# First norm's second step moved late, masks of v copied by ScalarE, and the raw loads of v put in order

## The chip, the cores and the metric

One core of a Trainium2 chip runs the whole program. The metric is the device time of one execution in microseconds (us). Engines are named as the profile names them: PE (matmuls) with PEld (its weight loads), DVE (VectorE), ACT (ScalarE), POOL (GpSimd), SP (SyncE, which here only issues transfers). PEclk is the clock granted to PE as a share of full speed.

## The reference

Four sequences of 576 tokens with 8 heads of 64 go through causal attention with a decay, then a normed MLP of 512 to 2048 to 512, then a gated spatial MLP. This case concerns the first two parts:

```
scores = scale * q @ k.T + (cum[:, None] - cum[None, :])      # cum: running sum of log f, causal mask
attn   = softmax(scores) @ v
xn     = (x - mean(x)) / sqrt(var(x) + 1e-06) * g_ln
x      = x + max(xn @ w_ch1, 0) @ w_ch2
```

The MLP's weights come as 64-bit numbers.

## The kernel before

Tokens are worked in blocks of 256 (`BLOCKS`), features on the partitions. Each block passes through an attention function (`attention32` for the first two blocks, `attention1` for the next two, `attention` later), a norm (`norm`) and the MLP (`mlp`); every block is an MLP group of its own here (group 0, group 1, ...). The MLP walks over `NF` = 16 weight blocks: a first product into `ph` (L840), a relu `hh` on ACT (L851), and a second product into the accumulators `acc` (L825), two weight blocks behind. There are 2 banks for `ph`, 2 for `acc`, 1 for `av`, and 3 buffers of `hh`.

Group 0 runs in f32 while its weights arrive: SP loads 64-bit words (`raw`, 3 buffers, L657 and L660), ACT and DVE narrow them (L641, L642 on ACT; L643, L644, L645 on DVE, the last into `wt`), PE adds up their squares (L692 into `gram`). From the squares `scales` derives scales (L710 to L716), and `make16` writes the weights as pairs of 16-bit parts (L723 on ACT, L726 on DVE). Groups from 1 on use these: their input is split into `xh` (L803, ACT) and `xl` (L804, DVE), and each product is made of three.

The norm of block 0 is cut in two. Its first step puts g and the mean into `xg0` (L755), from which group 0 can start. The second step (`self.rest`) finds the deviation: centring `xT` (L758), squares `sq` (L764 on ACT, summed by POOL in L768 and L769), a mean on PE (L736 into `av`), then `y` (L772, L773 on ACT and L774 to L776 on DVE). Group 0's products are multiplied by this `y` only at its end (L874), which also frees `acc` for group 1. `gscale` finds the scale `gs` of g that L803 and L804 use (L249 to L255).

A table of due positions (`REST`, `DEC`, `CONV`, ... in units of groups) sets in which order `run` writes the work. A scheduler in the framework then orders each engine's instructions; `self.after(later, earlier)` ties two of them in order, with `self.marks` for the named ones, and `high_priority` puts work first. In `attention32`, four steps `p` each make masks of scores (L440), an exponential (L442), a sum, a reciprocal and a diagonal matrix (L463 to L467), a transposing product (L473), and the product with `vm` (L485), which holds v twice under a mask. `attention1` runs eight units of scores (L518, L523, L525, L319, L534), a transfer that transposes (L535, `PT`<-`P`) and the product with v (L543 into `av`). `vnorm` loads v once more (`vraw`, L294 and L298) for its squares (L304).

Of the kernel before, what the change touches and what calls it, by code (L numbers as in the profile page):

```python
# [1 line left out]

# [4 lines left out]
F32 = mybir.dt.float32  # L7
# [6 lines left out]
AF = mybir.ActivationFunctionType  # L14
ALU = mybir.AluOpType
# [3 lines left out]
P = 128  # L19
# [6 lines left out]
TOK = 256  # L26
# [31 lines left out]
PACE = (1, "x3", "split", "split", "split")  # L58
LOWAT = (1, "x3", "split")
SUMS = 14  # L60
REST = 0.1
SQ = (1, 3, 4, 5, 6, 8, 9, 10, 12, 13, 14, 16)
SOON = 5
WSC, MAKE, VN = 0.76, 0.765, 0.82
# [24 lines left out]
class Kernel:  # L89
# [126 lines left out]
    def decays32(self, behind):  # L216


        nc, cum, lg, n = self.nc, self.cum, self.lg, B * H
        added = nc.vector.tensor_tensor(out=lg[:, P : P + 1], in0=lg[:, P : P + 1], in1=cum[:, P - 1 : P], op=ALU.add)  # L220
        self.after(added, behind)
        ones = self.ones[:n, :1].broadcast_to([n, S - P])
        return nc.vector.tensor_tensor_scan(out=cum[:, P:], data0=ones, data1=lg[:, P:], initial=0.0, op0=ALU.mult, op1=ALU.add)

    def decays16(self):

# [169 lines left out]
    def attention32(self, b, xT):  # L396
        nc, at, bufs = self.nc, self.at, BUFS0
        mm = nc.tensor.matmul

        def bank(tag):  # L400
            return self.bank(tag).rearrange("p (b u w) -> p b u w", b=2, u=2)

        def four(tag):
            return at.tile([P, 2, 2, P], F32, tag=tag, name=tag, bufs=bufs[tag])

        tags = ("s2", "s2", "av") if b else ("acc", "ph", "av")
        qka = self.qka0 if not b else at.tile([P, NP, 2, 2, 2 * P], F32, tag="qk", name="qk", bufs=bufs["qk"])
        vra = at.tile([P, 2, DM], F32, tag="vr", name="vr", bufs=bufs["vr"])
        vm = self.vm
        loads = []  # L410
        for p in range(NP):
            loads.append(nc.sync.dma_start(out=qka[:64, p], in_=self.qk0[b : b + 2, p].rearrange("n d u s -> d u n s")))
            if b and p == 1:
                for r in range(2):
                    row = qka[64 + r : 65 + r].rearrange("r p u n s -> r (p u n) s")
                    nc.sync.dma_start(out=row, in_=self.decay[b * H : (b + 2) * H, r])
        loads.append(nc.sync.dma_start(out=vra, in_=self.v[b : b + 2, :P].rearrange("b p d -> p b d")))
        for u in range(2):
            us = slice(64 * u, 64 * u + 64)
            v = vra.rearrange("p n (q w) -> p n q w", w=P)  # L420
            nc.gpsimd.tensor_copy(out=vm[:, :, :, u, us], in_=v[:, :, :, us])
        if b == 0:
            for x, y in zip(loads, loads[1:]):
                self.after(y, x)
            self.marks["loads"] = loads[-1]
        yield

        def scores(p):
            qk = qka[: 66 if b else P, p]
            ps, e = bank("s2" if p > 1 else tags[0]), four("e")  # L430
            st = at.tile([P, 2, 4], F32, tag="st", name="st", bufs=bufs["st"])
            for n, u, c in four_:
                ins = mm(ps[:, n, u], lhsT=qk[:, u, n, :P], rhs=qk[:, u, n, P:], start=True, stop=True, skip_group_check=True)
                if b and p == c == 0:
                    self.after(ins, self.first)
            if not b and p % 2:
                self.fill(FILLS[p // 2], ins)
            for n, u, c in four_:
                mn, sm = st[:, 0, c : c + 1], st[:, 1, c : c + 1]
                masked = nc.vector.tensor_tensor_reduce(  # L440
                    out=e[:, n, u], in0=ps[:, n, u], in1=self.mask[:, 512:], scale=-0.125, scalar=3e38, op0=ALU.add, op1=ALU.min, accum_out=mn)
                ex = nc.scalar.activation(e[:, n, u], e[:, n, u], AF.Exp, bias=mn, scale=-1.0, accum_out=sm)  # L442
                if b:
                    self.after(masked, self.marks["third" if p else "second"])
                    self.after(ex, self.marks["split"])
            if b:
                nc.scalar.activation(st[:, 1], st[:, 1], AF.Copy, bias=1e-9)
                nc.vector.reciprocal(st[:, 1], st[:, 1])
            else:
                self.masked = masked  # L450
            return e, st

        four_ = [(n, u, 2 * n + u) for n in range(2) for u in range(2)]
        ahead = []
        for p in range(NP):
            for i in range(len(ahead), min(p + 2, NP) if b else NP):
                ahead.append(scores(i))
                yield
            e, st = ahead[p]

            ps, pt, diag = bank(tags[1]), four("PT"), four("diag")
            if not b:
                total = nc.vector.tensor_scalar(out=st[:, 1], in0=st[:, 1], scalar1=1e-9, scalar2=None, op0=ALU.add)  # L463
                self.after(total, self.masked)
                self.masked = None
                nc.vector.reciprocal(st[:, 1], st[:, 1])
            drawn = nc.vector.tensor_tensor(  # L467
                out=diag.rearrange("p n u w -> p (n u) w"), in0=self.ident.unsqueeze(1).broadcast_to([P, 4, P]),
                in1=st[:, 1].unsqueeze(2).broadcast_to([P, 4, P]), op=ALU.mult)
            if not b:  # L470
                self.masked = drawn if p != 1 else self.decays32(drawn)
            for n, u, c in four_:
                ins = mm(ps[:, n, u], lhsT=e[:, n, u], rhs=diag[:, n, u], start=True, stop=True, skip_group_check=True)  # L473
            if not b and p < NP - 1:
                self.fill(FILLS[2], ins)
            if b or p % 2:
                copied = nc.scalar.activation(pt, ps, AF.Copy)
            else:
                copied = nc.vector.tensor_copy(out=pt, in_=ps)
            if not b:  # L480
                self.done.append(copied)
                self.marks[f"PT{p}"] = copied
            pav = bank(tags[2] if b else ("av", "s2", "acc", "s2")[p])
            for n, u, c in four_:
                ins = mm(pav[:, 0, n], lhsT=vm[:, n, p, u], rhs=pt[:, n, u], start=u == 0, stop=u == 1, skip_group_check=True)  # L485
            if not b and p == NP - 1:
                self.fill(FILLS[3], ins)
            copied = nc.scalar.activation(xT[:, p].rearrange("p (n w) -> p n w", n=2), pav[:, 0], AF.Copy)
            if not b:
                nc.scalar.activation(self.xg0[:, p].rearrange("p (n w) -> p n w", n=2), pav[:, 0], AF.Copy, scale=self.gT[:, p : p + 1])  # L490
            self.marks.setdefault(f"x{p}", copied)
            if p == 1:
                xs = self.mo_sum(xT)
            elif p == 2:
                nc.vector.tensor_tensor(out=xs, in0=xs, in1=xT[:, 2, :], op=ALU.add)
            yield
        return xs
# [166 lines left out]
    def load_w(self, j):  # L664

        nc = self.nc
        if j not in self.raw:
            self.load_raw(j)
        raw, w = self.raw.pop(j), self.wt[:, j + 2]
        low = self.st.tile([P, 2 * DM], U32, tag="low", name="low", bufs=2)  # L670
        joined = self.joined if 0 < j < 4 else None
        for hf in range(1 if j else 2):
            c = slice(0, 2 * DM) if j else slice(hf * DM, hf * DM + DM)
            first = self.narrow(raw[:, c], w[:, c], low[:, c], self.marks["split"] if hf else joined if j else self.marks["PT2"])
            for ins, pace in ((first, PACE), (self.low, LOWAT)):
                at = "x3" if hf else pace[j] if j < len(pace) else NP + j - len(pace) if ins is first else None
                if at is not None:
                    self.after(ins, self.marks[at] if isinstance(at, str) else self.done[at])
        if j == 1:
            self.marks["second"] = self.joined  # L680
        if j == 2:
            self.marks["third"] = self.joined

# [55 lines left out]
    def norm(self, x, s, y, whole, end, c):  # L739
# [11 lines left out]
        if c is not x:  # L751
            self.fill(FILLS[4], self.averaged)
            for t in range(NK):
                xg = self.xg0[:, t]
                self.marks["split"] = nc.vector.scalar_tensor_tensor(out=xg, in0=pm, scalar=self.gN[:, t : t + 1], in1=xg, op0=ALU.mult, op1=ALU.add)  # L755
            yield
        for t in range(NK):
            centred = nc.vector.tensor_tensor(out=c[:, t, :], in0=x[:, t, :], in1=pm, op=ALU.subtract)  # L758
# [667 lines left out]
```

## Time and profile before

| | us |
|---|---|
| median of 3 runs (lowest, highest) | 781.63 (781.2, 781.8) |
| the profiled execution | 784.81 |
| span of its trace | 782.8 |

| engine | busy us | share of the span |
|---|---|---|
| PE | 752.6 | 96% |
| DVE | 557.2 | 71% |
| ACT | 522.2 | 67% |
| POOL | 70.5 | 9% |

The span runs from the first to the last instruction; the execution took 2.0 us more. The profiled execution is 3.2 us above the median of the runs. A busy share is a mean over stages that differ much, so the stage that a change touches has to be read by itself. Times of records overlap by a little: an ACT record of 0.71 us, say, can be followed by the next one 0.61 us after its start.

### The profile page before, as it was taken

What the parts mean: (1) busy time and instruction counts of PE and PEld (TensorE: products, weight loads), DVE (VectorE), ACT (ScalarE), POOL (GpSimd) and SP (SyncE); (2) the same over time, 40 slices, a digit from 0 to 9 for tenths busy, and PEclk for the clock granted to TensorE, in tenths of its full rate; (3) what the DMA queues carried; (4) which work ended last, traced back from release to release, by engine and by line L of the source; (5) the groups of instructions that cost most, each with busy time, mean ns of one, the idle gap of its engine ahead of it and who ended that gap; (6) DMA issues with size and microseconds to landing.
All of it is one profiled execution on the core that took longest, in us unless ns stands there. A gap on an engine that the chain in (4) does not pass through costs nothing.

```text
span 782.8 us, 16313 instructions
## 1 busy us (share of the span) xinstructions
PE 752.6 (96%) x5966; PEld 578.3 (74%) x5966; DVE 557.2 (71%) x1508; ACT 522.2 (67%) x1317; POOL 70.5 (9%) x104
## 2 busy tenths in 40 slices
PE   7889998999999989999999999999999999999998
PEld 6778877877877867778888888544447678668676
DVE  7899698667599889979869946587525672654624
ACT  6888598667588888878759834485416743756543
POOL 5210101012101001110101100100021000000000
PEclk9999998999999999999999999999999999999999
DMA  9968994266679998987994955730034310100101
GB/s 256 279 239 284 296 182 77 55 189 102 186 154 202 183 207 152 211 198 153 178 204 108 132 80 196 192 118 29 1 80 75 102 63 1 39 23 17 47 1 61
DMA packets 164099, 104.69 MB, mean 134 GB/s; under 512 B 106146, under 2 KB 151298, under 8 KB 164020
## 3 DMA queue, kind: packets, MB, share of 16 engines
q1 hardware_dynamic: 157784, 96.60, 51.2%
q0 software_dynamic: 5376, 5.54, 5.0%
q10 hardware_dynamic: 860, 1.52, 0.6%
q8 instruction: 47, 0.77, 0.4%
q14 instruction: 32, 0.26, 0.1%
HBM read 64.37 MB, written 15.11 MB: 102 GB/s over the span
## 4 chain that ended last, share of the span: by engine, by line
PE 61%; DVE 13%; DMA 11%; ACT 8%; issue 4%; SPq 1%; POOL 1%; ACTq 0%; DVEq 0%; POOLq 0%
PE ph L840 14%; PE acc L825 12%; PE pb L785 8%; PE pb L786 8%; PE pb L784 8%; PE s L359 3%; DMA raw<-in_moe_w_ch_dram 3%; DMA vr<-in_v_dram 3%; PE av L570 3%; DMA PT<-P 2%; PE s L825 1%; DVE wt L726 1%; DVE x2z L342 1%; DVE P L380 1%; ACT low L642 1%
## 5 line engine op out<-in xcount | busy, mean ns | idle before, releaser
L825 PE MATMUL acc<-hh,wt 128*128 128x256 f16 (+2 forms) x960 | 196.8, 295 | 3.0 <-ACT hh L851 1.9
L840 PE MATMUL ph<-xh,wt 128*128 128x256 f16 (+1 forms) x896 | 186.3, 290 | 4.4 <-DVE hl L855 4.2
L840 PEld LDWEIGHTS <-wt 128*128 128x128 f16 x1344 | 127.5, 98 | 50.9 <-issue 13.1
L825 PEld LDWEIGHTS <-wt 128*128 128x128 f16 x1344 | 129.2, 98 | 43.9 <-issue 5.9
L840 PE MATMUL ph<-xl,wt 128*128 128x256 f16 (+1 forms) x448 | 129.5, 289 | 0.0
L825 PE MATMUL acc<-hl,wt 128*128 128x256 f16 (+1 forms) x416 | 115.3, 281 | 0.8 <-DVE hl L855 0.8
L851 ACT ACTIVATE hh<-ph 128x256 f16<-128x256 f32 (+2 forms) x128 | 50.9, 397 | 52.4 <-PE ph L840 52.0
L855 DVE SCALAR_TENSOR_TENSOR hl<-ph,hh 128x256 f16<-128x256 f32 (+1 forms) x112 | 50.8, 455 | 38.8 <-ACT hh L851 38.3
L319 ACT ACTIVATE P<-sd,st 128x512 f16<-128x512 f32 (+2 forms) x128 | 70.4, 586 | 11.3 <-DVE st L370 5.6
L380 DVE SCALAR_TENSOR_TENSOR P<-sd,st,P 128x384 f16<-128x384 f32 (+2 forms) x96 | 58.0, 623 | 9.0 <-ACT P L319 8.1
L367 ACT ACTIVATE sd<-sd,st 128x384 f32<-128x384 f32 (+2 forms) x80 | 54.6, 682 | 11.9 <-DVE st L363 11.6
L876 POOL DMA_DIRECT2D x_d<-t x36 | 32.0, 1053 | 204.3 <-DVE t L872 167.0
L359 PE MATMUL s<-x2z 128*128 128x384 f32 (+3 forms) x128 | 47.3, 379 | 1.4 <-DMA x2z<-decay_d 1.4
L363 DVE CUSTOM_DVE_ANT_0 sd<-s,mask 128x384 f32<-128x384 f32 (+2 forms) x80 | 45.9, 578 | 2.9 <-PE s L359 1.9
L359 PE MATMUL s<-x 128*128 128x384 f32 (+3 forms) x128 | 41.3, 332 | 0.0
L1152 DVE SCALAR_TENSOR_TENSOR u<-pb,wsc,u 128x288 f32<-128x288 f32 x32 | 16.1, 515 | 34.5 <-PE pb L1151 34.5
L784 PE MATMUL pb<-x2h,wil 128*128 128x288 f16 (+2 forms) x144 | 37.8, 273 | 0.0
L785 PE MATMUL pb<-x2l,wih 128*128 128x288 f16 (+2 forms) x144 | 37.7, 273 | 0.0
L786 PE MATMUL pb<-x2h,wih 128*128 128x288 f16 (+2 forms) x144 | 37.7, 273 | 0.0
L784 PE MATMUL pb<-wsh,vl 128*128 128x288 f16 x128 | 36.6, 286 | 0.1
L786 PE MATMUL pb<-wsh,vh 128*128 128x288 f16 x128 | 36.6, 286 | 0.0
L785 PE MATMUL pb<-wsl,vh 128*128 128x288 f16 x128 | 36.6, 286 | 0.0
(301 smaller groups left out, 1662.4 us busy)
## 6 DMA issues: line engine op xcount, KB each, us to landing
raw<-in_moe_w_ch_dram SPq DMA_DIRECT2D x32, 512.0 KB
qk<-in_qk_dram SPq DMA_DIRECT2D x32, 448.0 KB
vraw<-in_v_dram SPq DMA_DIRECT2D x5, 1024.0 KB
vr<-in_v_dram SPq DMA_DIRECT2D x16, 320.0 KB
x_d<-xT SPq DMA_DIRECT2D x9, 512.0 KB
x_d<-t POOLq DMA_DIRECT2D x36, 128.0 KB, 4.2
out_dram<-o SPq DMA_DIRECT2D x32, 144.0 KB
raw<-in_moe_w_in_dram SPq DMA_DIRECT2D x8, 512.0 KB
```

What stands on the lines that cost most here:

```text
L319: self.nc.scalar.activation(out, in_, AF.Copy, scale=scale)
L359: nc.tensor.matmul(ps[: R * u + R, : c1 - c0], lhsT=x[:, lo - q0 - R * u : hi - q0], rhs=y[:, c0:c1], start=g == 0, stop=g == len(heads[u] ...
L363: nc.vector.tensor_tensor_reduce(out=sd[:M, c0:c1], in0=ps[:M, : c1 - c0], in1=mask, scale=-0.125, scalar=3e38 if n == 0 else st[:M, n - 1 ...
L367: nc.scalar.activation(sd[:M, :N], sd[:M, :N], AF.Exp, bias=st[:M, n : n + 1], scale=-1.0, accum_out=st[:M, 2:3])
L380: low = nc.vector.scalar_tensor_tensor(out=dl, in0=src, scalar=rs, in1=dh, op0=ALU.mult, op1=ALU.subtract)
L784: first = mm(out, lhsT=al, rhs=bh, start=start, stop=False, **kw)
L785: mm(out, lhsT=ah, rhs=bl, start=False, stop=False, **kw)
L786: mm(out, lhsT=ah, rhs=bh, start=False, stop=stop, **kw)
L825: ins = nc.tensor.matmul(acc[m], lhsT=a, rhs=b, start=bank not in clear, stop=last and e == len(terms) - 1, skip_group_check=True)
L840: ins = nc.tensor.matmul(ph, lhsT=a, rhs=b, start=k == e == 0, stop=k == NK - 1 and e == len(terms) - 1)
L851: relu = nc.scalar.activation(hh, ph, AF.Relu)
L855: nc.vector.scalar_tensor_tensor(out=hl, in0=ph, scalar=0.0, in1=hh, op0=ALU.max, op1=ALU.subtract)
```

## The change

- `REST` goes from 0.1 to 0.7, so the second step of block 0's norm and `gscale` are written late in group 0. As the mean's bank would be held until then, ACT copies it into a tile `kept`, from which the centring reads.
- In the second block's `attention32`, the two copies of v into `vm` are done by ACT, behind the second half of the third weight block's narrowing (`low2`), and no longer by POOL.
- Sums, reciprocals and diagonals become a function `norms`. In the first block, step 0's is done before the masks of step 3. In the second block masks and diagonals get a higher priority, and the diagonal stands right behind the reciprocal.
- The second part of the decays' running sum (`decays32`, L220 and L223) moves from among the first block's diagonals to behind the first narrowing.
- The mark that `load_w` set as "second" is called "w1" now. Before, `attention1`'s own mark of that name, set only where there was none, had no effect; now it has, and the loads of `vraw` that refer to it come behind the second of `attention1`'s loads of v.

```diff
-REST = 0.1
+REST = 0.7
...
-            nc.gpsimd.tensor_copy(out=vm[:, :, :, u, us], in_=v[:, :, :, us])
+            if b:
+                self.after(nc.scalar.activation(vm[:, :, :, u, us], v[:, :, :, us], AF.Copy), self.marks["low2"])
+            else:
+                nc.gpsimd.tensor_copy(out=vm[:, :, :, u, us], in_=v[:, :, :, us])
...
+                with self.tc.high_priority(1) if b else nullcontext():
+                    masked = nc.vector.tensor_tensor_reduce(
...
-                    self.after(masked, self.marks["third" if p else "second"])
+                    self.after(masked, self.marks["third" if p else "w1"])
...
+                if not b and i == NP - 1:
+                    ahead[0] = norms(*ahead[0])
...
-                self.masked = drawn if p != 1 else self.decays32(drawn)
...
+            if j == hf == 0:
+                self.decays32(self.joined)
...
+        self.marks[f"low{j}"] = self.low
         if j == 1:
-            self.marks["second"] = self.joined
+            self.marks["w1"] = self.joined
...
+            kept = ns.tile([P, TOK], F32, name="kept")
+            self.after(nc.scalar.activation(kept, pm, AF.Copy), self.marks["split"])
+            pm = kept
```

The lines of the changed kernel are numbered up to 18 higher; where its rows are shown below, the text gives the number of before.

On ACT, `y` of block 0 (L772, L773) stood early in group 0, among the narrowing:

```order
L764 ACTIVATE sq<-xT 128x1024
L851 ACTIVATE hh<-ph 128x256
L442 ACTIVATE e,st<-e,st 128x128 x4
L641 ACTIVATE wt<-raw 128x1024
L447 ACTIVATE st<-st 128x4
L772 ACTIVATE y<-av,eps 128x256
L773 ACTIVATE y<-y 128x256
L642 ACTIVATE low<-raw 128x1024
```

In the changed kernel it stands behind the split of group 1's input and behind 16 of the copies that make 16-bit weights (L738, before L723); L790 and L791 are before's L772 and L773, L869 is the relu and L537, L280, L538, L319 belong to `attention1`:

```order
L869 ACTIVATE hh<-ph 128x256
L537 ACTIVATE sd,st<-sd,st 128x256
L280 ACTIVATE vp<-vr,vs 128x256
L790 ACTIVATE y<-av,eps 128x256
L738 ACTIVATE wt<-wt,w1c 128x512
L738 ACTIVATE wt<-wt,w2c 128x512
L869 ACTIVATE hh<-ph 128x256
L280 ACTIVATE vp<-vr,vs 128x256
L538 ACTIVATE st<-st 128x2
L738 ACTIVATE wt<-wt,w1c 128x512
L738 ACTIVATE wt<-wt,w2c 128x512
L791 ACTIVATE y<-y 128x256
```

From the split (its first row, L821, not shown) to L791 there are now 4 of `xh`, 20 copies of weights and 20 others: 3 each of L544, L272, L280 and L851, 4 of L525, 2 of L526, `sq` and L772.

On DVE, the end of group 0's accumulators (L874) stood soon behind the split of group 1 (L804); these rows begin right behind the split:

```order
L726 SCALAR_TENSOR_TENSOR wt<-wt,w1c 128x512
L726 SCALAR_TENSOR_TENSOR wt<-wt,w2c 128x512
L523 ISA sd,st<-s_1121,mask 128x256
L263 TENSOR_SCALAR vs<-vs 128x1
L874 TENSOR_TENSOR t<-y,acc 128x256 x2
...
L874 TENSOR_TENSOR t<-y,acc 128x256 x2
```

Now block 0's centring (L776, before L758) stands inside the split (L822, before L804), and 22 weights (L741, before L726) and the masks of three units of attention (one before) come behind the split before `acc` is freed. These rows end at the first of the weights:

```order
L796 TENSOR_TENSOR xT<-xT,y 128x1024
L546 SCALAR_TENSOR_TENSOR P_1032<-sd,st,P_1032 128x2x128 x2
L822 SCALAR_TENSOR_TENSOR xl<-xT,gs,xh 128x256
L776 TENSOR_TENSOR xT<-xT,kept 128x256 x4
L822 SCALAR_TENSOR_TENSOR xl<-xT,gs,xh 128x256 x3
L741 SCALAR_TENSOR_TENSOR wt<-wt,w1c 128x512
```

On SP, the first load of `vraw` (L294) stood ahead of `attention1`'s loads (L509 to L511), and three of the other four ahead of the transposes (L535) of its second and third unit:

```order
L660 DMA raw<-in_moe_w_ch_dram 128x512
L294 DMA vraw<-in_v_dram 128x4x512
L509 DMA qk<-in_qk_dram 64x768
...
L294 DMA vraw<-in_v_dram 128x4x512
L535 DMA_TRANSPOSE PT<-P_981 128x8x128
L298 DMA vraw<-in_v_dram 128x4x512
L535 DMA_TRANSPOSE PT<-P_1057 128x8x128
```

Now three of them stand together behind the third unit's loads (L523, before L511), and the last behind the third transpose (L547, before L535):

```order
L523 DMA vr<-in_v_dram 128x2x128
L294 DMA vraw<-in_v_dram 128x4x512 x3
...
L547 DMA_TRANSPOSE PT<-P_956 128x8x128
L294 DMA vraw<-in_v_dram 128x4x512
L547 DMA_TRANSPOSE PT<-P_1032 128x8x128
L298 DMA vraw<-in_v_dram 128x4x512
```

PE's rows are in step with these: group 1's first product L840 stood behind the third unit's L543, and now stands ahead of it; its first L825 stood behind the products of 2 weight blocks, and now behind those of 5 and behind the fourth unit's L543.

## Rows read from the trace of the kernel before

**Rows 1.** The page: the chain that ended last, by engine.

```profile
PE 61%; DVE 13%; DMA 11%; ACT 8%; issue 4%; SPq 1%; POOL 1%; ACTq 0%; DVEq 0%; POOLq 0%
```

**Rows 2.** Windows: stretch, length, busy of each engine, PEclk, DMA share, GB/s.

```profile
44.00:72.00 28.00, 28.00 (x196) 25.28 (x197) 27.44 (x53) 25.15 (x49) 0.57 (x1) 1.00 0.74 257
116.00:120.00 4.00, 0.46 (x10) 0.47 (x12) 4.00 (x13) 3.97 (x11) 2.06 (x3) 0.91 0.96 99
120.00:124.00 4.00, 4.00 (x22) 2.97 (x19) 2.97 (x10) 3.31 (x8) 1.53 (x2) 0.50 1.00 118
124.00:128.00 4.00, 4.00 (x38) 3.44 (x37) 1.53 (x3) 1.76 (x6) 0.00 (x0) 0.74 0.31 84
140.00:240.00 100.00, 96.69 (x888) 79.97 (x887) 71.76 (x214) 67.42 (x193) 10.48 (x13) 1.00 0.63 142
240.00:340.00 100.00, 93.81 (x862) 76.57 (x862) 87.51 (x238) 83.50 (x220) 10.80 (x17) 0.98 1.01 193
```

**Rows 3.** Groups on PE, 24 to 44 us: busy, mean ns, idle before and its releaser.

```profile
L825 PE MATMUL acc<-hh,wt 128*128 128x256 f32 x24 | 5.8, 386 | 1.2 <-ACT hh L851 1.2
L692 PE MATMUL gram<-wt 128*128 128x128 bf16 x24 | 2.0, 219 | 1.7 <-DVE wt L645 1.7
L736 PE MATMUL av<-sq,onesf 128*128 128x256 f32 x1 | 0.5, 483 | 1.7 <-POOL sq L769 1.7
```

**Rows 4.** DVE's timeline, 14 to 53 us: start, length, instruction, idle before.

```profile
14.35 1.08 DVE L223 TENSOR_TENSOR_SCAN cum<-ones,lg 32x448 f32<-32x448 f32 x1
...
24.02 1.66 DVE L755 SCALAR_TENSOR_TENSOR xT<-av,gN,xT 128x256 f32<-128x256 f32 x4 [1.42 <-PE av L736]
...
33.55 1.22 DVE L645 SCALAR_TENSOR_TENSOR wt<-wt,low 128x1024 uint32<-128x1024 uint32 x1
34.69 1.40 DVE L758 TENSOR_TENSOR xT<-xT,av 128x256 f32<-128x256 f32 x4
...
36.61 0.67 DVE L251 TENSOR_REDUCE gmax<-gall 128x1 f32<-128x512 f32 x1
...
41.08 2.21 DVE L645 SCALAR_TENSOR_TENSOR wt<-wt,low 128x1024 uint32<-128x1024 uint32 x1
...
43.28 1.68 DVE L645 SCALAR_TENSOR_TENSOR wt<-wt,low 128x1024 uint32<-128x1024 uint32 x1
...
52.43 0.42 DVE L776 SCALAR_TENSOR_TENSOR y<-t,y 128x256 f32<-128x256 f32 x1
```

**Rows 5.** POOL's timeline, 20 to 46 us.

```profile
28.29 2.82 POOL L421 COPY vm<-vr 128x512 f32<-128x512 f32 x2 [16.00 <-DMA vr<-in_v_dram]
...
39.95 2.25 POOL L768 TENSOR_TENSOR sq<-sq 128x512 f32<-128x512 f32 x1 [7.29 <-ACT sq L764]
42.28 1.59 POOL L769 TENSOR_TENSOR sq<-sq 128x256 f32<-128x256 f32 x1
```

**Rows 6.** ACT's timeline, at 44 us and from 111 us.

```profile
44.66 0.47 ACT L772 ACTIVATE y<-av,eps 128x256 f32<-128x256 f32 x1 [1.86 <-PE av L736]
...
111.35 1.69 ACT L803 ACTIVATE xh<-xT,gs 128x256 f16<-128x256 f32 x4
...
117.88 0.71 ACT L723 ACTIVATE wt<-wt,w2c 128x512 f16<-128x512 f32 x1
118.49 0.50 ACT L280 ACTIVATE vp<-vr,vs 128x256 f16<-128x256 f32 x1
118.89 0.50 ACT L525 ACTIVATE sd<-sd,st 128x256 f32<-128x256 f32 x1
```

**Rows 7.** PE's timeline, 107 to 136 us.

```profile
112.00 0.53 PE L543 MATMUL av<-PT,vp 128*64 128x128 f16 x12
...
119.54 0.85 PE L543 MATMUL av<-PT,vp 128*64 128x128 f16 x12 [3.62 <-DMA PT<-P]
...
135.75 0.27 PE L840 MATMUL ph<-xh,wt 128*128 128x256 f16 x1
```

**Rows 8.** SP's timeline: the issue of the second unit's transpose.

```profile
107.81 1.26 SPq L535 DMA_TRANSPOSE PT<-P  x1
```

More of the change, by code (lines that the diff above doesn't have):

```diff
@@ L1 @@
-from contextlib import ExitStack
+from contextlib import ExitStack, nullcontext
 import concourse.bass as bass
@@ L222, in decays32 @@
         ones = self.ones[:n, :1].broadcast_to([n, S - P])
-        return nc.vector.tensor_tensor_scan(out=cum[:, P:], data0=ones, data1=lg[:, P:], initial=0.0, op0=ALU.mult, op1=ALU.add)
+        nc.vector.tensor_tensor_scan(out=cum[:, P:], data0=ones, data1=lg[:, P:], initial=0.0, op0=ALU.mult, op1=ALU.add)
     def decays16(self):
@@ L439, in scores, with norms @@
                 mn, sm = st[:, 0, c : c + 1], st[:, 1, c : c + 1]
-                masked = nc.vector.tensor_tensor_reduce(
-                    out=e[:, n, u], in0=ps[:, n, u], in1=self.mask[:, 512:], scale=-0.125, scalar=3e38, op0=ALU.add, op1=ALU.min, accum_out=mn)
+                with self.tc.high_priority(1) if b else nullcontext():
+                    masked = nc.vector.tensor_tensor_reduce(
+                        out=e[:, n, u], in0=ps[:, n, u], in1=self.mask[:, 512:], scale=-0.125, scalar=3e38, op0=ALU.add, op1=ALU.min, accum_out=mn)
                 ex = nc.scalar.activation(e[:, n, u], e[:, n, u], AF.Exp, bias=mn, scale=-1.0, accum_out=sm)
                 if b:
-                    self.after(masked, self.marks["third" if p else "second"])
+                    self.after(masked, self.marks["third" if p else "w1"])
                     self.after(ex, self.marks["split"])
[L446 to L449, printed above, removed]
+                if not b and p == NP - 1:
+                    self.after(masked, self.drawn)
+            if not b:
                 self.masked = masked
             return e, st
+        def norms(e, st):
+            diag = four("diag")
+            with self.tc.high_priority(1) if b else nullcontext():
+                if b:
+                    nc.scalar.activation(st[:, 1], st[:, 1], AF.Copy, bias=1e-9)
+                else:
+                    total = nc.vector.tensor_scalar(out=st[:, 1], in0=st[:, 1], scalar1=1e-9, scalar2=None, op0=ALU.add)
+                    self.after(total, self.masked)
+                nc.vector.reciprocal(st[:, 1], st[:, 1])
+                drawn = nc.vector.tensor_tensor(
+                    out=diag.rearrange("p n u w -> p (n u) w"), in0=self.ident.unsqueeze(1).broadcast_to([P, 4, P]),
+                    in1=st[:, 1].unsqueeze(2).broadcast_to([P, 4, P]), op=ALU.mult)
+            if not b:
+                self.drawn = self.masked = drawn
+            return e, diag
         four_ = [(n, u, 2 * n + u) for n in range(2) for u in range(2)]
@@ L456, in attention32 @@
             for i in range(len(ahead), min(p + 2, NP) if b else NP):
+                if not b and i == NP - 1:
+                    ahead[0] = norms(*ahead[0])
                 ahead.append(scores(i))
                 yield
[L459 to L470, printed above, removed]
-                self.masked = drawn if p != 1 else self.decays32(drawn)
+            if b or p:
+                ahead[p] = norms(*ahead[p])
+            e, diag = ahead[p]
+            ps, pt = bank(tags[1]), four("PT")
             for n, u, c in four_:
```

## The prediction

> **What bounds the kernel now.** I read the chain of waits first. By engine it is PE for 61% of the span, then DVE, DMA and ACT with 13, 11 and 8 [rows 1]: PE is the bound in most stages, and a change of other engines' work counts only where PE waits for them. So I looked for PE's holes. There are three places. In 24 to 44 us PE stands still for 1.7 us until a weight block is narrowed, 1.7 us until POOL has summed the squares of block 0, and 1.2 us for a relu, 4.6 us together [rows 3]; right behind that, from 44 to 72 us, it is full with 28.00 of 28 [rows 2]. At the turn from group 0 to group 1, PE works 0.46 of 4 us, then finds a clock of 0.50 for 4 us and 0.74 for the next 4 [rows 2]; the reason is the third unit's transpose, for which L543 waits 3.62 us in front of everything else in PE's queue [rows 7]. The third place is long: 3.3 us are missing in 140 to 240 and 6.2 in 240 to 340 [rows 2], in which DVE is busy with 72 and then 88 of 100 us.
>
> **The start of group 0 (gain).** Four things get shorter.
> First, the scan of 1.08 us leaves the first block's diagonals and stands now where DVE waits 1.42 us for the mean [rows 4]. That wait is its cover; if it were gone, it would cost its 1.08. With the sums of step 0 in front of the last masks, the first block ends an estimated 1.6 us sooner: the scan, and what DVE does in a wait for PE.
> Second, DVE gets rid of work while it is full: centring 1.40, the maximum of g 0.67 and some five short ones (an estimated 0.5 together), and three steps of y at 0.42, 3.8 us in all [rows 4]. All of it is moved and none of it is removed.
> Third, POOL's sums ran at 39.95 and 42.28 for 2.25 and 1.59 us [rows 5], and in that time two L645 took 2.21 and 1.68 instead of 1.22 [rows 4], an excess of 1.45. The sums move to the turn, where DVE makes the weights (L726) without a pause, so I count the excess as a gain here and as a load there, where I find it covered (below). The Trainium skill (SBUF — State Buffer, "Who interferes with whom") says that a VectorE instruction with two SBUF inputs and a GpSimd one that reads SBUF share a port as an exclusive lock, so that one waits for the whole of the other. L645 has two such inputs and its two durations agree with that; by the rule alone the excess would not be saved but only moved, since L726 has two as well, and the sum would be the same as mine.
> Fourth, ACT stood 1.86 us waiting for this mean [rows 6], with the next L642 queued behind it, and for that L642 waits L644, which frees a buffer of `raw`.
> Against these, ACT gets the copy into `kept` and two copies of v. POOL took 2.82 us for the two [rows 5]; ACT passes 512 elements in 0.61 [rows 6], so they cost 1.2 there, and 0.3 for `kept`, bounds 0 (in an idle moment) and 1.5.
> How much of this reaches the end of group 0? At least the 1.6 of the first block. At most that and all of DVE's 3.8 and 1.45 with ACT's 1.86, 8.7. PE's own holes allow 4.6 and 1.6, so 6.2. The loads are released by DVE and ACT, so they follow; they could hold some of it back. I take 5.0: PE's 6.2 less ACT's new 1.2.
>
> **The turn to group 1 (loss).** I count from the start of the split of xh, 111.35 us before [rows 6], which comes 5.0 sooner. There PE's order changes most. Group 1's first product is no longer behind the third transpose; but the first L825 now stands behind five weight blocks of first products and the fourth unit's L543, and it needs the accumulators, which L874 frees only when y is there.
> ACT must do 4 of xh (1.6 us), 20 copies at 0.61 (12.2) and 21 others before y is done, L773 counted. The others take 0.25 to 0.5 from start to start, as L280 with 0.40 [rows 6], sq about 0.95; I take 8.0 for them. That is 21.8, and 0.9 for L544, whose product hangs on the third transpose (8.2 us behind the start of xh, [rows 6, 7]). DVE has to do the rest of the split, the centring and some 20 L726 first, an estimated 22 by the same count; it keeps level with ACT, and so 0.7 us of DVE's excess by POOL is covered by ACT.
> So y's last steps start at 22.7 us. Of the fourth unit two steps L534 follow them (1.2 with L774), then its transpose: the second unit's was issued at 107.81 and used at 112.00, 4.2 us [rows 7, 8]. With 1.7 for L543 and the scores behind it, the first L825 starts 29.9 us behind the start of xh; 28.2 if only L874 counted.
> Before, as much work on PE was behind it at 135.75 [rows 7], 24.4 us after the start of xh: by then first products of 4 blocks and 26 matmuls of the second had run, 74 matmuls at 0.11; now it is 60, one mean and one more unit of attention, which is worth the same to 0.3 us. So the new order costs 29.9 less 24.4, 5.5 us. Bounds: 3.8 by L874 alone, and 9.1 if the fourth transpose is as late as the third was, 3.62 more [rows 7].
> Then the clock. PE has only some 15 us of work in these 30, and most of a stretch of 7 us before the fourth L543 is empty. After a stretch like that the clock was 0.50 and 0.74 for 4 us each, which is 3.0 us of work [rows 2]. In the old order this is counted within the 24.4, and in the new one it comes again, behind L825. I take 2.5, bounds 0 and 3.0.
>
> **What comes back.** At the same state of PE, ACT and DVE will have done some 8 us more of their work (all 16-bit weights, one more unit), so they are ahead of PE when group 2 and the larger attention units come. PE's 9.5 us of holes in 140 to 340 [rows 2] are waits for just that kind of work. I take 4.0, as the attention of these groups hangs on transfers too; bounds 0 and 9.5.
>
> **Sum.** 5.0 less 5.5 less 2.5 and 4.0 again: a gain of 1.0. From 784.81 us of the profiled execution, 783.8. The median of the runs is 3.2 below the profiled execution, so I predict 780.8; from the median of 781.63 that is a gain of 0.1%. What a measurement can tell from no change is 0.2%, 1.6 us, so "the same" is 780.1 to 783.2.
>
> **Rivals.**
> 1. The forecast: early gain and late y cancel to a few us, 778.5 to 783.5. Chance 0.42; of this 0.14 is faster and 0.25 the same.
> 2. Faster. PE goes on with attention while L825 waits, the transposes are quick since loads of `vraw` no longer stand among them, and the holes behind close by most of their 9.5 us. With 5.0 and a return of 8.5 against 5.5 and 2.5 it is a gain of 5.5, so 776. For it: DVE and ACT are full at the turn, so no time of theirs is lost. Against it: in 140 to 240 DVE has 28 of 100 us free and PE 3.3, so being ahead there has little to fill. Chance 0.27.
> 3. Slower. L874 is late, PE runs out of work, and nothing of it comes back: 5.0 less 5.5 less 3.0, a loss of 3.5, so 785. It decides from the point where the first L825 starts later than 29 us behind xh while PE in 140 to 340 has as many holes as before. For it: only 2 banks of `ph` and 3 buffers of `hh`, so PE can't take more first products ahead, and 140 to 240 is full already. Chance 0.26.
> 4. The change does nothing early: the 3 buffers of `raw` and the loads set the pace, the narrowing ends at the same time, and only the first block's 1.6 stays. Then 1.6 less 5.5 less 2.5 and 4.0 gives a loss of 2.4, 784. Against it: L644, which frees a buffer, is itself late by DVE and ACT at 40 to 47 us. Chance 0.05.
>
> Faster by over 0.2%: 0.14 and 0.27, 0.41. The same: 0.25, and 0.03 of the others, 0.28. Slower: 0.31. The range goes from the fast rival to the slow one with its late transposes, 774.8 to 786.8.
>
> **What the changed profile would show.** L755 starts about 1.6 us sooner than at 24.02. No wait for POOL's sums between 24 and 44 us, L645 at 1.22 there, and PE's holes gone. The split of xh at 106 to 107. L773 22 to 23 us behind it, L874 at 28, the first L825 at 30, with a wait on PE of several us before it and a clock of 0.5 behind. PE in 140 to 340 with 5 to 6 us of holes instead of 9.5. The prediction would be wrong if the split came less than 3 us sooner, if y were done much before 22 us, or if PE's holes behind 140 us all stayed or all closed.

## The result and the profile after

The changed kernel takes 785.19 us (median of 5 runs, 784.56 to 786.87), the kernel before 781.2 (778.69 to 781.8): a ratio of 1.0059, 95% interval 1.0038 to 1.0079. It is slower by 4 us. I had predicted 780.8, no change to speak of, and had given 0.31 to slower. The profiled execution of the changed kernel took 784.56, 0.6 below its median; that of the kernel before had taken 784.81, 3.2 above the median of its runs.

Windows of the changed kernel at the turn and behind it (columns as in [rows 2]):

```profile
116.00:120.00 4.00, 3.47 (x29) 2.99 (x28) 4.00 (x13) 4.00 (x12) 0.00 (x0) 1.00 0.21 60
120.00:124.00 4.00, 2.19 (x17) 1.64 (x16) 4.00 (x13) 4.00 (x13) 0.00 (x0) 1.00 0.08 25
124.00:128.00 4.00, 3.68 (x19) 2.69 (x19) 4.00 (x12) 4.00 (x10) 0.00 (x0) 0.57 0.11 33
128.00:132.00 4.00, 0.77 (x7) 0.42 (x5) 4.00 (x12) 1.20 (x4) 0.00 (x0) 0.93 0.34 65
132.00:136.00 4.00, 2.58 (x17) 2.16 (x18) 3.81 (x14) 2.42 (x11) 2.33 (x3) 0.50 0.57 90
136.00:140.00 4.00, 4.00 (x18) 2.47 (x17) 2.01 (x9) 2.67 (x8) 1.29 (x2) 0.50 1.10 142
140.00:144.00 4.00, 4.00 (x46) 3.03 (x45) 1.11 (x3) 1.53 (x5) 0.00 (x0) 0.79 0.67 100
140.00:240.00 100.00, 97.63 (x905) 80.51 (x905) 70.23 (x205) 66.94 (x191) 10.50 (x13) 0.99 0.66 146
240.00:340.00 100.00, 95.36 (x886) 78.27 (x886) 85.34 (x233) 83.19 (x217) 10.83 (x17) 1.00 1.00 192
```

DVE has 4.00 of 4 us from 116 to 132, and PE 0.77 in 128 to 132: PE waits while DVE works. Twice the clock falls, and at 136 to 144 it costs work, since PE is busy all the time at 0.50 and 0.79. Where PE waits, its timeline says for what:

```profile
124.32 0.27 PE L858 MATMUL ph<-xh,wt 128*128 128x256 f16 x1 [2.12 <-DVE vs L263]
...
132.56 0.85 PE L555 MATMUL av<-PT,vp 128*64 128x128 f16 x12 [3.79 <-DVE P L546]
134.27 0.59 PE L274 MATMUL s<-vq,ones 128*128 128x1 f32 x2 [0.86 <-ACT vp L272]
134.72 2.06 PE L530 MATMUL s<-qk 66*128 66x256 f32 x4
136.57 0.42 PE L843 MATMUL acc<-hh,wt 128*128 128x256 f16 x1
```

L843 at 136.57 is the first second-product of group 1; L555 is the fourth unit's product with v. The row names L546 on DVE for its wait. The weight load of the same product names the transposing transfer behind it (waits, 120 to 140 us):

```profile
PEld L555 <- DMA PT<-P: 4.1, 1, 4.1
```

That transfer was issued at 129.45, right behind the L546 of 128.55, which stands on DVE behind y's first step. So the wait that ends last at this turn is the fourth unit's; the accumulators, freed from 132.97 on, matter through PE's order, in which L843 stands behind L555, L274 and L530 (e5 shows what happens when it need not). DVE's timeline in the same stretch:

```profile
110.63 1.61 DVE L741 SCALAR_TENSOR_TENSOR wt<-wt,w1c 128x512 f16<-128x512 f32 x1
112.16 1.22 DVE L741 SCALAR_TENSOR_TENSOR wt<-wt,w2c 128x512 f16<-128x512 f32 x1
...
128.22 0.42 DVE L792 SCALAR_TENSOR_TENSOR t<-av,y 128x256 f32<-128x256 f32 x1
128.55 0.87 DVE L546 SCALAR_TENSOR_TENSOR P<-sd,st,P 128x256 f16<-128x256 f32 x2
...
132.97 0.73 DVE L892 TENSOR_TENSOR t<-y,acc 128x256 f32<-128x256 f32 x2
```

ACT's timeline gives the start of group 1's split and y's last step there:

```profile
104.22 1.71 ACT L821 ACTIVATE xh<-xT,gs 128x256 f16<-128x256 f32 x4 [0.47 <-DVE xT L796]
...
125.47 0.43 ACT L791 ACTIVATE y<-y 128x256 f32<-128x256 f32 x1
```

The split starts 7.1 us sooner than in [rows 6], but y's last step on ACT starts only 21 us behind it and its last on DVE 28 us behind it, the accumulators are freed from 132.97 on, and the lead is gone. At the start, the groups on PE in 24 to 44 us answer to [rows 3]; the wait for POOL is no longer there, and the other two, 2.9 us before, are 2.8 (all of PE's holes in that stretch: 4.8 before, 2.8 now, so they did not close as forecast):

```profile
L843 PE MATMUL acc<-hh,wt 128*128 128x256 f32 x24 | 6.0, 392 | 2.2 <-ACT hh L869 2.2
L707 PE MATMUL gram<-wt 128*128 128x128 bf16 x32 | 2.7, 219 | 0.6 <-DVE wt L657 0.6
```

### The profile page after: what moved, and what is told of

Same layout as the page of the kernel before. It is cut to its first block, busy times and chain, and to the rows that moved or that the text cites. A ratio compares the mean times of both kernels' runs of the same rounds, so it can differ in the third digit from the quotient of the medians.

```text
span 782.6 us, 16305 instructions
## 1 busy us (share of the span) xinstructions
PE 754.1 (96%) x5966; PEld 578.2 (74%) x5966; DVE 558.3 (71%) x1508; ACT 524.1 (67%) x1320; POOL 67.7 (9%) x102
## 4 chain that ended last, share of the span: by engine, by line
PE 52%; DVE 15%; ACT 13%; issue 13%; DMA 6%; POOL 1%; SPq 0%; ACTq 0%; DVEq 0%; POOLq 0%
PE ph L858 11%; PE acc L843 11%; PE pb L803 7%; PE pb L804 7%; PE pb L802 7%; PE s L359 3%; PE av L582 3%; ACT wt L738 2%; DMA raw<-in_moe_w_ch_dram 1%; DVE x2z L342 1%; DVE sd L363 1%; ACT P L319 1%; ACT x L319 1%; DVE P L380 1%; ACT sd L367 1%
## 5 line engine op out<-in xcount | busy, mean ns | idle before, releaser
L843 PE MATMUL acc<-hh,wt 128*128 128x256 f16 (+2 forms) x960 | 198.3, 297 | 4.7 <-ACT hh L869 4.5
L843 PEld LDWEIGHTS <-wt 128*128 128x128 f16 x1344 | 130.2, 99 | 47.0 <-issue 8.3
L858 PE MATMUL ph<-xl,wt 128*128 128x256 f16 (+1 forms) x448 | 129.7, 290 | 0.0
L843 PE MATMUL acc<-hl,wt 128*128 128x256 f16 (+1 forms) x416 | 116.2, 283 | 0.5 <-DVE hl L873 0.5
L869 ACT ACTIVATE hh<-ph 128x256 f16<-128x256 f32 (+2 forms) x128 | 50.8, 398 | 55.5 <-PE ph L858 54.8
L319 ACT ACTIVATE P<-sd,st 128x512 f16<-128x512 f32 (+2 forms) x128 | 70.7, 587 | 8.0 <-DVE st L370 4.3
L804 PE MATMUL pb<-x2h,wih 128*128 128x288 f16 (+2 forms) x144 | 37.7, 273 | 0.0
L804 PE MATMUL pb<-wsh,vh 128*128 128x288 f16 x128 | 36.6, 286 | 0.0
```

The costliest lines, as they stand in the source:

```text
L319: self.nc.scalar.activation(out, in_, AF.Copy, scale=scale)
L804: mm(out, lhsT=ah, rhs=bh, start=False, stop=stop, **kw)
L843: ins = nc.tensor.matmul(acc[m], lhsT=a, rhs=b, start=bank not in clear, stop=last and e == len(terms) - 1, skip_group_check=True)
L858: ins = nc.tensor.matmul(ph, lhsT=a, rhs=b, start=k == e == 0, stop=k == NK - 1 and e == len(terms) - 1)
L869: relu = nc.scalar.activation(hh, ph, AF.Relu)
```

## The experiments

Theory "late y": the change brings the narrowing forward, but y of block 0 is now done behind the copies of 16-bit weights; group 0's accumulators are held, group 1's second products can't start, PE runs dry. Rival "other parts": masks of v on ACT, the moved loads or the moved scan cost the time. Rival "load": the moved work itself loads DVE and ACT at the turn, whoever holds the accumulators. The kernel before was measured beside each of them (column "before"); ratios are to it, with 95% intervals, and are not simply the quotient of the two medians:

| | kernel | median us | before | ratio |
|---|---|---|---|---|
| e1 | before, again | 782.03 | 781.34 | 1.0013 (0.9989 to 1.0037) |
| e2 | changed, REST 0.1 | 780.09 | 781.34 | 0.9984 (0.9962 to 1.0007) |
| e3 | changed, REST 0.4 | 781.53 | 781.34 | 1.0004 (0.9980 to 1.0029) |
| e4 | changed, REST 0.6 | 778.01 | 781.34 | 0.9966 (0.9946 to 0.9987) |
| e5 | changed, accumulators freed without y | 777.47 | 781.05 | 0.9955 (0.9932 to 0.9977) |
| e6 | changed, y ahead of copies from block 7 | 775.09 | 781.05 | 0.9919 (0.9895 to 0.9942) |
| e7 | before, raw loads of v moved | 779.63 | 781.05 | 0.9993 (0.9970 to 1.0017) |
| e8 | before, REST 0.7 with kept | 784.91 | 781.05 | 1.0062 (1.0036 to 1.0087) |
| e9 | as e6, from block 9 | 782.42 | 783.15 | 0.9983 (0.9962 to 1.0005) |
| e10 | as e6, from block 5 | 782.74 | 783.15 | 0.9988 (0.9966 to 1.0010) |
| e11 | e5 and e6 together | 779.49 | 783.15 | 0.9951 (0.9934 to 0.9968) |
| e12 | as e6, masks of v by POOL | 778.25 | 783.15 | 0.9947 (0.9925 to 0.9968) |

Each of e1 to e12 was executed 11 or 12 times, e6 only 6 times. Single executions of one kernel lie far apart here: 35 of the kernel before, made beside e1 to e4, went from 777.45 to 785.72. The time goes with the clock: the 16 of them with a mean granted clock of 0.993 or less took 783.1 on average, the 16 with 0.996 or more 779.9.

From each trace I took six points: the start of group 1's split (first `xh`, on ACT), the end of PE's last f32 product of group 0 (L825 by the lines of before), and the ends of DVE's last product with the accumulators (L874 or L872) of groups 0, 1, 2 and 6. They come from one execution each, and two of these were long ones: e8's took 790.04, 5.1 above its median, and e12's 780.65, 2.4 above.

| us | split of group 1 | PE's group 0 | end of group 0 | group 1 | group 2 | group 6 |
|---|---|---|---|---|---|---|
| before | 111.3 | 115.1 | 119.3 | 189.5 | 246.4 | 495.7 |
| e1, before again | 110.4 | 114.7 | 118.4 | 187.2 | 244.1 | 493.8 |
| changed | 104.2 | 109.8 | 134.9 | 190.2 | 249.4 | 496.3 |
| e2 | 104.8 | 115.3 | 119.3 | 186.0 | 245.0 | 491.9 |
| e3 | 105.0 | 112.6 | 117.8 | 180.9 | 245.6 | 495.4 |
| e4 | 105.3 | 110.6 | 131.9 | 187.0 | 242.4 | 490.4 |
| e5 | 104.2 | 109.8 | 111.9 | 183.8 | 242.8 | 490.4 |
| e6 | 104.3 | 109.7 | 126.3 | 182.8 | 238.3 | 486.5 |
| e7 | 108.9 | 114.5 | 116.8 | 184.5 | 241.7 | 490.7 |
| e8 | 101.9 | 113.7 | 138.7 | 194.9 | 257.2 | 502.3 |
| e9 | 104.5 | 110.3 | 130.1 | 186.2 | 245.1 | 494.5 |
| e10 | 104.6 | 111.7 | 124.9 | 189.3 | 247.6 | 497.2 |
| e11 | 104.6 | 110.2 | 112.2 | 183.9 | 241.1 | 491.1 |
| e12 | 107.6 | 113.1 | 129.7 | 189.3 | 244.3 | 492.7 |

The split, from which the prediction counts, is no measure of PE's lead. The other parts of the change alone (e2) bring it 5.6 us forward from e1, and PE ends group 0 no sooner than before; the late step alone (e8) brings it 8.5 us forward, and PE gains 1.0; with both, PE gains 4.9. PE's last f32 products in the kernel before, the changed one, e2 and e8, in this order:

```profile
113.65 1.46 PE L825 MATMUL acc<-hh,wt 128*128 128x256 f32 x6
106.13 3.67 PE L843 MATMUL acc<-hh,wt 128*128 128x256 f32 x16
112.88 2.40 PE L840 MATMUL acc<-hh,wt 128*128 128x256 f32 x10
110.00 3.67 PE L828 MATMUL acc<-hh,wt 128*128 128x256 f32 x16
```

### e1: the kernel before once more

No edit.

> The kernel before, unchanged, profiled once more. The first profiled execution took 784.81 us, 3.2 above the median of the unprofiled ones, and I carried that distance over to the changed kernel, whose profiled execution (784.56) turned out 0.6 below its own median (785.19). If the distance was an accident of that one execution, the new profile takes 779 to 782, its turn from group 0 to group 1 is shorter, and the third unit's L543 waits clearly less than 3.62 us for its transpose. If a profile makes the old kernel slower and the new one not, it takes 784 to 786 again, with the same wait. Ratio to the kernel before: 1.000 within 0.002.

The profiled execution took 781.67, and L543's wait for its transpose was 2.85 instead of 3.62. PE's timeline of this run:

```profile
118.31 0.53 PE L543 MATMUL av<-PT,vp 128*64 128x128 f16 x12 [2.85 <-DMA PT<-P]
...
133.08 0.27 PE L840 MATMUL ph<-xh,wt 128*128 128x256 f16 x1
```

The row that stood at 135.75 in [rows 7], my reference for the turn, stands at 133.08 here, 2.7 us sooner of the 3.1 by which this execution is shorter. So the distance to the median was mostly an accident of one turn. The wait itself is shorter by 0.8 only, less than I expected; 1.4 is the shorter stretch at the low clock behind it, and PE was 0.5 sooner before the wait.

### e2, e3 and e4: REST 0.1, 0.4 and 0.6

```diff
-REST = 0.7
+REST = 0.1
...
-            kept = ns.tile([P, TOK], F32, name="kept")
-            self.after(nc.scalar.activation(kept, pm, AF.Copy), self.marks["split"])
-            pm = kept
```

e3 and e4 keep the copy and set 0.4 and 0.6.

> The changed kernel with block 0's second norm step and g's scale early again (REST 0.1, no kept copy); all other parts stay. Theory late y: y comes in time, the first second-product of group 1 stands behind 3 first products again, and the turn's loss goes; of the early gain of 7.1 us at the split of group 1's input some 4 go back too (DVE's work returns to 24 to 54 us), so 777 to 780. Rival other parts: the loss comes from v's masks on ACT, from the moved loads or from the moved scan, and stays: 784 to 786.

> The changed kernel with REST 0.4 in place of 0.7: the step stays out of 24 to 54 us, but on ACT y of block 0 is done right behind the split of group 1's input (2 copies of weights before it, not 20), and 9 weights on DVE stand before the end of the accumulators, not 22. Theory late y: early gain of 6 to 7 us kept, no wait of PE for the accumulators, first L843 some 20 us behind the split's start (32.3 in the changed kernel): 774 to 778. Rival other parts: 784 to 786.

> The changed kernel with REST 0.6: on ACT 16 copies of weights and 11 other instructions stand behind the split before y is done (20 and 20 at 0.7), on DVE 20 weights before the accumulators are freed (22 at 0.7); 5 first products still stand before the first second-product. Theory late y: only a part of the loss goes, by the 7 us less of ACT's work at most: 780 to 784, between REST 0.4 and 0.7. Rival other parts: no dependence on REST, 784 to 786.

With REST 0.1 all other parts of the change stay, and the loss is gone: 780.09, 5.1 us below the changed kernel. "Other parts" falls as the cause of the loss. The early gain is gone with it: the split came at 104.8, only 0.6 later than with the step late, but PE ended group 0 at 115.3 instead of 109.8. e3 missed its 774 to 778. It frees the accumulators at 117.8 and ends group 1 at 180.9, 9.3 us ahead of the changed kernel, and 5.5 of that are gone by the end of group 2: from 160 to 240 us PE was busy 73.84 us of 80 (77.63 in the changed kernel) at a granted clock of 0.96 (1.00), and group 2's split came no sooner (224.2 against 223.2). e4, with 16 copies and 11 other instructions on ACT before y (20 and 20 in the changed kernel), was better than the 780 to 784 I gave: its accumulators came free only 3.0 us sooner, and it is 7 us faster. So the time isn't a line in REST from 0.1 to 0.7. That each value gives another order everywhere is my explanation, which no run tests.

### e5: the accumulators freed, y as late

```diff
-                    else:
-                        nc.vector.tensor_tensor(out=t[:, m], in0=y, in1=a, op=ALU.mult)
+                    else:
+                        nc.vector.tensor_copy(out=t[:, m], in_=a)
+                if not g:
+                    nc.vector.tensor_tensor(out=t[:, m], in0=y, in1=t[:, m], op=ALU.mult)
```

> The changed kernel (REST 0.7, y as late as there), but group 0's end first copies the accumulators to SBUF on DVE as they are and multiplies by y there, so that group 1's second products need no y to start; 4 more DVE instructions of 0.33. Theory late y: what costs is that the accumulators are held; the first second-product of group 1 starts over 8 us sooner than its 136.6, PE's clock does not fall a second time, and the time comes to that of REST 0.1, 778 to 781. Rival load: the work moved to the turn loads DVE and ACT there whoever holds the accumulators; 784 to 786.

DVE copies the accumulators at once, and PE's first second-product stands at 117.47 (136.57 in the changed kernel); rows of DVE and of PE:

```profile
110.48 1.41 DVE L892 COPY t<-acc 128x256 f32<-128x256 f32 x4
```

```profile
117.47 0.38 PE L843 MATMUL acc<-hh,wt 128*128 128x256 f16 x2
```

The clock stays at 1.00 from 100 to 160 us, and the time is 777.47, a little better than the 778 to 781 I gave. The split starts at 104.2 and PE ends group 0 at 109.8, both as in the changed kernel, and y is nearly as late (18 copies and 18 others before it); DVE even has more to do. So "load" falls, and what costs is that the accumulators wait for y. The fourth unit's L555 is no sooner here (133.19), but PE has second products to do ahead of it. L843 19 us sooner is not a lead of 19 us: only two weight blocks of first products and three units stand before it, five and four in the changed kernel. By the end of group 1 the lead is 6.4 us, by group 6 5.9, and the time is 7.7 less. From 160 to 240 us PE has 74.38 of 80, 3.3 less than the changed kernel.

### e6: y ahead of the copies

```diff
+        grown = nc.scalar.activation(y, y, AF.Exp, scale=-0.5)
+        if c is not x:
+            self.grown = grown
...
+            if j >= SOON + 2:
+                self.after(ins, self.grown)
```

> The changed kernel with one more order on ACT: the copies of 16-bit weights from the seventh weight block on stand behind y of block 0. Behind the split 4 copies and 19 others come before y is done (20 and 20 in the changed kernel), on DVE 8 weights before the accumulators are freed (22). Theory late y: the accumulators are free some 8 us sooner than at 134.9, and the time is 777 to 781. Rival load: 784 to 786. If the copies, now later, are missed by group 1's products, it ends in between, 781 to 784, with waits of PE for weights.

775.09, 10 us below the changed kernel, the best of all and below the 777 to 781 I gave: 0.9919 of the kernel before. The accumulators are free at 126.3, 8.6 sooner, and by the end of group 1 all but 1.2 of it is left, by group 6 it has grown to 9.8. No other part of the change was undone.

### e7 and e8: one part alone

e7 is the kernel before with the mark renamed:

```diff
-                    self.after(masked, self.marks["third" if p else "second"])
+                    self.after(masked, self.marks["third" if p else "w1"])
...
-            self.marks["second"] = self.joined
+            self.marks["w1"] = self.joined
```

e8 is the kernel before with REST 0.7 and the three lines on `kept`.

> The kernel before with the raw loads of v put behind attention1's loads alone (the mark renamed), nothing else. With REST 0.1 in the changed kernel the split of group 1's input started at 104.8, 5.6 us sooner than the 110.4 of the kernel before, though block 1 was centred at 88.0 in both; so the step that was moved late had little to do with it. Theory loads: attention1's first loads of v no longer wait behind the raw ones (ACT waited 4.3 us for them at 87 to 92 us); the split starts at 105 to 107 and the time is 778 to 781. Rival: the gain came from the first block's order and v's masks on ACT; the split stays at 109 to 111, the time at 781 to 783.

> The kernel before with block 0's second norm step and g's scale late alone (REST 0.7 with the kept copy), nothing else. Theory late y: it costs here too, 785 to 789, as the accumulators are freed behind 24 weights on DVE (4 before). Rival: the loss needs the other parts, which fill ACT and DVE at the turn; 780 to 783. The split of group 1's input shows what the moved work itself buys: 1 us or less sooner than 110.4 if the raw loads set its time, 4 us or more if DVE's load did.

e7's split is at 108.9, 1.5 sooner than in e1 and short of the 105 to 107 of the theory, and by the ratio its time can't be told from that of before. The theory that the loads bring the early gain falls: ACT still waits for v's loads, 3.6 us instead of 4.3 (waits of ACT, 80 to 100 us):

```profile
ACT vp L272 <- DMA vr<-in_v_dram: 3.6, 2, 2.8
```

e8 has the earliest split of all profiles, 101.9, and the latest accumulators, 138.7, and is slower by 0.62%, as much as the whole change. Its turn alone costs: from PE's end of group 0 to the first second-product (L828 at 139.09) it takes 25.4 us, 26.8 in the changed kernel, and 18.4 in e1 to the row at 133.08. So the late step needs no other part to cost at the turn. Not all of e8's loss is the turn, though: with POOL still copying the masks, PE waits 3.1 us at a stretch for narrowing between 24 and 44 us, and the granted clock is 0.91 there (1.00 in the changed kernel). DVE's timeline of e8, where L877 is L874 of before:

```profile
135.34 0.42 DVE L779 SCALAR_TENSOR_TENSOR y<-t,y 128x256 f32<-128x256 f32 x1
...
137.22 0.42 DVE L877 TENSOR_TENSOR t<-y,acc 128x256 f32<-128x256 f32 x1
```

### e9 to e11: how much sooner, and both together

e9 has `SOON + 4` in e6's condition, e10 `SOON`; e11 is e6 with the edit of e5.

> As the version with y ahead of the copies, but only from the ninth weight block on: 8 copies and 20 others on ACT before y is done (4 and 19 there, 20 and 20 in the changed kernel), 14 weights on DVE before the accumulators are freed (8 there, 22 in the changed kernel). Theory late y: the time stands between the two, 778 to 782, with the accumulators free at 129 to 132. Rival: the gain of 10 us came from something else in that order, not from when y is done; then 774 to 777 or 784 to 786 without a place between.

> As the version with y ahead, from the fifth copied weight block on, all copies behind the split stand behind y: 0 copies before y, 3 weights on DVE before the accumulators are freed. Theory late y: the accumulators are free at 122 to 125 and the time is 773 to 776, at or below the 775.1 of the version with 4 copies. Rival copies: the weights are missed now, PE waits for L741 or ACT's L738 in group 1's products, and it is 776 to 780.

> The version with y ahead of the copies (from the seventh block) and the accumulators copied out before y. If they cost only by being held, this adds what is left: 3 first products before the first second product instead of 4, 772 to 775. If, with y in time, the wait left at the turn is that for attention, it adds nothing: 774.5 to 777, the time ahead given back in 160 to 240 us, as the version with free accumulators alone did.

e9 lies between, as expected: 0.9983, with the accumulators at 130.1 (782.42 is just outside the 778 to 782, beside a kernel before that took 2 us longer than beside e6). e10 doesn't follow: accumulators at 124.9, sooner than e6, and 0.9988. PE's waits in it, 120 to 200 us, of which e6 has only 0.4 for `qk` (its longest is 2.9 for `hl`):

```profile
PE av L555 <- DMA PT<-P: 2.0, 1, 2.0
PE s L530 <- DMA qk<-in_qk_dram: 1.7, 1, 1.7
PE vgram L314 <- DVE vss L312: 1.6, 1, 1.6
```

These are attention's transfers and v's squares, not the weights that I had named as its rival. Why they come later in this order, I haven't tried. PE also ends group 0 2.0 us later than in e6, has 10.8 us of holes from 140 to 340 (7.6), and its granted clock in that stretch is 0.97 (1.00). So three orders that differ by a few copies lie 0.7% apart, more than the loss that is to be explained. e11, 0.9951, adds nothing to e6 and ends where e5 alone did, as the second answer that I gave for it says, though at 779.49 it lies above both bands. In e3, e5 and e11, where the second products start soonest, PE stands still for 5 to 6 of the 80 us from 160 to 240: a lead in the MLP at the turn is in part given back there.

### e12: masks of v by POOL again

```diff
-            if b:
-                self.after(nc.scalar.activation(vm[:, :, :, u, us], v[:, :, :, us], AF.Copy), self.marks["low2"])
-            else:
-                nc.gpsimd.tensor_copy(out=vm[:, :, :, u, us], in_=v[:, :, :, us])
+            nc.gpsimd.tensor_copy(out=vm[:, :, :, u, us], in_=v[:, :, :, us])
```

> The version with y ahead, but the second block's v copied into its masks by POOL again (2.82 us for two in the kernel before). Theory: in 24 to 44 us DVE and ACT are the full engines; ACT saves 1.2 us, DVE's L657 beside the copy takes 1.5 instead of 1.22, so the effect is under 2 us either way: 774 to 777. Rival: POOL's late copy holds the second block up; narrowing ends 2 us or more later, 777 to 780.

0.9947 against e6's 0.9919; the intervals overlap, so the 2 us between them aren't certain. In the trace the split comes at 107.6, 3.3 later, PE ends group 0 3.4 later, and it waits for narrowing at the start where e6 has 0.6 us of it; the group on PE, 24 to 44 us:

```profile
L705 PE MATMUL gram<-wt 128*128 128x128 bf16 x27 | 2.8, 244 | 3.3 <-DVE wt L655 3.3
```

The rival's mechanism is there (the last narrowing starts at 84.55 instead of 81.49), and the granted clock from 24 to 44 us is 0.83 (1.00 in e6). So at the start ACT's copies are worth more than the 1.2 us that I booked as a cost; what is left of it in the time isn't certain.

## Why the prediction was wrong

**The start (right at PE's end of group 0).** I took 5.0 us. The split of group 1 came 7.1 sooner than in [rows 6] and 6.2 sooner than in e1, but PE's last f32 product came 5.3 and 4.9 sooner, which is the number that counts. L645 took 1.19 to 1.23 throughout, and POOL's sums no longer stop PE; but PE's holes between 24 and 44 us went from 4.8 only to 2.8. L755 came 0.8 sooner, not 1.6, as a copy of transposed attention weights (L491, L479 before) waited 1.69 us for PE there, 0.77 before. That the moved step is the source of the gain is half right: alone it brings PE 1.0 (e8), and the other parts without it bring nothing (e2). With POOL's copies of v back PE loses 3.4 of the gain (e12), so the two need each other.

**POOL's excess moved (right).** Two L741 took 1.61 and 1.22 beside POOL's sums (1.62 and 1.06 at 110.06 and 111.76) and 0.74 otherwise, 1.35 us together; 1.45 were saved early. The Trainium skill (SBUF — State Buffer, "Who interferes with whom") says that a VectorE instruction with two SBUF inputs contends with a GpSimd one that reads SBUF, by an exclusive lock. The trace agrees: each of the two ends 0.56 us behind POOL's, and each of the slow L645 in [rows 4] ended 1.09 behind the sum beside it in [rows 5].

**The turn (right in its mechanism, too small).** y's last step on ACT 21.2 us behind the split instead of 22.7, L892 at 28.7 instead of 28.2, L555 at 28.3: as counted. But from L555 to L843 I took 1.7, and it was 4.0, since L274 waited 0.86 for ACT and L530 ran at the low clock (2.06 us). The first L843 stood 32.3 us behind the split, not 29.9. As the split was sooner than I took it, the two misses cancel: by my sum L843 was due at 136.25, and it came at 136.57.

**The reference of before and the 3.2 us (the step that failed).** I measured the turn against 135.75 in one profiled execution, 24.4 us behind its split. In e1 it is 133.08 less 110.4, 22.7. So the new order costs 32.3 less 22.7, 9.6 us, not 5.5: 2.4 from what follows L555, 1.7 from the reference. (Counted from PE's end of group 0 instead, the gain is 4.9 and the cost 26.8 less 18.4, 8.4.) And then I took 3.2 off the sum as the distance of that execution to the median. But e1 shows that distance to be mostly its slow turn, which the changed kernel doesn't have: it was counted once as a turn that is easy to beat, and once more as an offset. In terms of the profiled execution the sum gave 783.8, and the changed kernel's took 784.56. So of the miss of 4.4 us, 0.8 is the terms of the sum, 3.2 the offset and 0.6 the distance of the changed kernel's profile to its own median, less 0.2, as 783.8 less 3.2 is 780.6 and not 780.8. Left at 783.8, the sum would have said slower. That e1's execution is the usual one rests on its lying 0.4 from its median; it is one execution.

**Clock and return.** The low clock behind L843 cost 2.6 (half of 136.57 to 140, and 0.21 of 4), as counted. Of what comes back I took 4.0; by e1 it is 3.0 at the end of group 1 (6.2 less 9.6 less 2.6 is a loss of 6.0, and 190.2 stands against 187.2), and about 0.5 more by group 6 (496.3 against 493.8). With these numbers, 6.2 less 9.6 less 2.6 and 3.0 is a loss of 3.0, and 784.56 against 781.67 is 2.9; as the 3.0 was itself found as what remained, this says only that little is won or lost behind group 1. Rival 3 named the right size, and its first condition held, the first L825 later than 29 us. But it said that nothing comes back, and PE's holes in 140 to 340 went from 9.5 us (8.7 in e1) to 7.0; so its 785 is in part luck, a smaller gain and a smaller loss with no return.

**Cause.** Shown: with the step late alone the kernel loses as much (e8), without it nothing is lost (e2), with y as late but the accumulators free it gains (e5), with y ahead of the copies it gains most (e6). The two kernels whose accumulators come free behind 134 us are the only slow ones; all the others, with 111.9 to 131.9, are at 1.0013 of the kernel before or below. Not shown: that the time grows with the lateness, since below 132 us the two have no order (117.8 and 1.0004, 131.9 and 0.9966). Nor how much of the gain of e4 and e6 over the kernel before is y's and how much the luck of an order. Open: why y at its earliest (e10) is no better than the kernel before, beyond the transfers that its waits name.

## What to carry to other kernels

Work that is moved off a crowded stretch has a consumer; look what that consumer holds meanwhile. Here a chain of some dozen small instructions, moved late, held two accumulator banks for 23 us (last product of group 0 done at 109.8, freed from 132.97), and the best cure of those tried was not to move it back but to order 18 copies behind it (22 did not help, e10). Count a lead where the engine that bounds the kernel ends its work: the split on ACT came 5.6 us sooner in e2 and PE had nothing of it. When a sum is made against one profiled execution, find out first whether its distance to the median sits in the very stage that the change touches: then it must not be taken off again.

## What the runs showed of the hardware that was not expected

One kernel's executions spread by 8.3 us (777.45 to 785.72), twice the effect in question, and more than the 3.1 between its two profiled executions, which differ mostly in one transfer and the clock behind it (3.62 and 2.85 us of wait; 135.75 and 133.08). The mean granted clock of an execution tells much of it: 783.1 on average at 0.993 or less, 779.9 at 0.996 or more. A short hole of PE is not paid once: in the changed kernel PE was granted 0.50 at 132 to 140 us after 0.77 busy us of the 4 at 128 to 132, and 0.79 in the 4 us behind.
